# One ordered list of small steps for the prelude and the first 16 units of a fused attention and FFN kernel

## The chip, the cores and the metric

The kernel runs on one core of one Trainium2 chip. The time is device microseconds of one execution. Engines are named as in the profile: PE is TensorE (PEld its weight loads), DVE is VectorE, ACT is ScalarE, POOL is GpSimd, SP is SyncE, which here issues the DMAs.

## What is computed

Batch 8, 8 heads, 512 local and 32 global tokens, head size 64; then an FFN over all 8 x 544 tokens, 512 to 2048 to 512, with a leaky activation that has its own slope for every hidden unit.

```python
k_all = concat([k_g, k_l]); v_all = concat([v_g, v_l])
out_g = softmax(scale * q_g @ k_all.T) @ v_all          # 32 global queries see all keys
s_ll  = where(abs(i - j) <= 32, scale * q_l @ k_l.T, -1e9)
s_l   = concat([scale * q_l @ k_g.T, s_ll])             # local: a window, and the 32 global keys
out_l = softmax(s_l) @ concat([v_g, v_l])
x = concat([out_g, out_l])                              # heads side by side: 512 columns
h = x @ w_in
g = maximum(h, 0) + alpha * minimum(h, 0)
out = g @ w_out
```

## The kernel before

**Units.** The FFN runs in groups of tokens: eight local groups of 512 tokens, one for each batch, and one of the 256 global tokens. A group is worked in 16 units, one for each block f of 128 hidden units. Unit T does `f1(T)`: 12 matmuls of 128x512 that make h for its block, then g (ACT takes the negative part, VectorE combines: "bend"), then a high part gh (ACT, rounded to fp32r) and a low part gl (POOL). `f2(T, 0)` multiplies gh with both parts of the weights (8 matmuls), `f2(T, 1)` multiplies gl with the high part (4 matmuls), both into four banks of PSUM, `LAG` = 2 units later. All operands of the FFN are split like this into a high and a low part.

**Weights.** They come as 64-bit floats, 1 MB for a block f, and are decoded on the chip once, during the first 16 units: `take_high` and `take_low` on ACT, `shift` (two instructions) and `join` (two) on VectorE, then `upper` on ACT (the rounded high part) and `lower` on VectorE (the rest). Unit f of the first group needs `lower(f)`. Three buffers of 128x1024 (`dec`) hold what is being decoded: one from `take_high` to `lower`, one from `take_low` to `join`.

**Attention.** Its local part goes by pairs of heads P, four pairs for each batch: `local_scores` on PE, `local_maxima` on VectorE, `local_exps` on ACT, `local_transposes` on PE with copies of the result, `local_values` on PE, `local_weights` (division by the sum) on VectorE, `local_outputs` (transposes) on PE. Pairs 0 to 3 make x of the first group and stand in a prelude. Pairs 4 to 7 make x of the second group and lie between the first group's units. From pair 8 on (`NRAW`) the transposition goes through a VectorE block transpose and DRAM instead (`local_exchange`). Global attention starts in the second group.

**What orders the work.** A planner orders the instructions by due times from its own timeline. PE's instructions are kept in program order throughout; those of ACT and VectorE are kept in it up to the end of the first group (`act.on`, `vec.on`), the DMAs of the start until `dma.on = False`. So in the prelude and the first group the program text is the order: first the prelude's calls one after the other (lines 542 to 595), then the loop of line 596, where each unit emits f1, g, the f2 of two units before, and the decode steps of later units (lines 612 to 620), and where `attention(t, where)` emits what was planned for that place. `keep_warm(n)` issues n matmuls on zeros into a bank of their own.

**Buffers that matter.** `st`: 21 tiles of 128x512 for x, g, p and so on. PSUM: two banks `h` (f1, values, outputs), two banks `s`, four banks `o0` to `o3` (scores in the prelude, f2 afterwards).

Of the kernel before, what the change touches and what calls it, by code (L numbers as in the profile page):

```python
# [18 lines left out]
NPAIR = 4  # L19
# [14 lines left out]
PAD = (64, 32)  # L34
LAG = 2
NRAW = 2 * NPAIR
NLOAD = 6
# [34 lines left out]
def longformer_ffn(ctx: ExitStack, tc: tile.TileContext, qk, vs, gn, vg, w, alpha, out):  # L72
# [45 lines left out]
    idle = stage("idle", F32R)  # L118
    vec.memset(idle.bitcast(F32), 0.0)
# [20 lines left out]
    def keep_warm(n, tag="s"):  # L140
        for _ in range(n):
            ps = bank(tag, "warm")
            matmul(ps, idle[:, 0:128], idle, start=True, stop=True)

    wslot, wmid, wts = {}, {}, {}
# [12 lines left out]
    def take_high(f):  # L158
        if f < NF:
            wmid[f] = [wide("wt"), None]  # L160
            act.activation(wmid[f][0], words(f)[1].bitcast(F32), AF.Abs)

    def take_low(f):
        if f < NF:
            wmid[f][1] = wide("wr", I32)
            act.activation(wmid[f][1], words(f)[0], AF.Copy, scale=2.0**-29)

    def shift(f):
        if f < NF:
            t = wmid[f][0]  # L170
            vec.tensor_scalar(t, t, CLAMP_LO, CLAMP_HI, op0=ALU.max, op1=ALU.min)
            tu = t.bitcast(U32)
            vec.tensor_scalar(tu, tu, 3, 0x3FFFFFFF, op0=ALU.logical_shift_left, op1=ALU.bitwise_and)

    def join(f):
        if f < NF:
            t, r = wmid[f]
            tu, ti = t.bitcast(U32), t.bitcast(I32)
            vec.scalar_tensor_tensor(tu, words(f)[1], 0xC0000000, tu, op0=ALU.bitwise_and, op1=ALU.bitwise_or)
            vec.tensor_tensor(ti, ti, r, op=ALU.add)  # L180
            del wslot[f]
            wmid[f] = t
# [35 lines left out]
    ps_of, pr_of, z_of, pt_of, xq_of = {}, {}, {}, {}, {}  # L218

    def local_scores(P):  # L220
        t = qks.pop(P)
        tags = ("o0", "o1", "o2", "o3") if P < NPAIR else ("s", "s", "s", "s")
        for h in range(2):
            ps_of[P, h] = bank(tags[2 * (P % 2) + h], "s_ps")
            if P < NRAW:
                matmul(ps_of[P, h], ident_bf, mask_bf, start=True, stop=False)
        for j in range(NWIN):
            c, wd = divmod(j, 4)
            i = place(P, c, wd)
# [21 lines left out]
    def local_exps(P):  # L251
        z_of[P] = small("z", 8)
        for h in range(2):
            src, mn, scale = ps_of.pop((P, h))
            p = pr_of[P, h] = stage("p") if P < NRAW else pr_of[P, h]
            for i in range(4):
                k = 2 * i + h
                act.activation(p[:, 128 * i : 128 * i + 128], src[:, i], AF.Exp, bias=mn[:, i : i + 1], scale=scale, accum_out=z_of[P][:, k : k + 1])

    def local_transposes(P):  # L260
        ps = {}
        for h in range(2):
            p = pr_of.pop((P, h))
            ps[h] = bank("s", "pt")
            for i in range(4):
                transpose(ps[h][:, 128 * i : 128 * i + 128], p[:, 128 * i : 128 * i + 128], ident)

        def put():
            for h in range(2):
                pt_of[P, h] = stage("pt")  # L270
                copy("d" if P < NPAIR else "a", pt_of[P, h], ps[h])

        if P < NPAIR:
            return put
        put()
# [22 lines left out]
    def local_values(P):  # L298
        o = bank("h", "o_ps")
        v = vws.pop(P)  # L300
# [8 lines left out]
    def local_weights(P):  # L309
        o, z, rz = ps_of.pop(P), z_of.pop(P), small("rz", 8)  # L310
        act.activation(rz, z, AF.Copy, bias=1e-9)
# [8 lines left out]
    def local_outputs(P):  # L320
        xq = xq_of.pop(P)
        ps = bank("h", "xt")
        for i in range(4):
            transpose(ps[:, 128 * i : 128 * i + 128], xq[:, 128 * i : 128 * i + 128], ident)
        if P < NPAIR:
            return lambda: xs.update({(0, P): split(ps, SL)})
        act.copy(x_raw[:, P % NPAIR], ps)
# [16 lines left out]
    def global_scores(k):  # L344
# [11 lines left out]
        m, z = small("gm", 4), small("gz", 4)  # L356
# [52 lines left out]
    gs, obs = {}, {}  # L409

    def f1(T, after=None, between=None):
        G, f = divmod(T, NF)
        n = SL if GROUPS[G][0] == "l" else NB * SG
        h = bank("h", "h_ps")
# [9 lines left out]
        g = stage("g")  # L424
        act.activation(g[:, 0:n], h[:, 0:n], AF.Relu, scale=-1.0)
        vec.scalar_tensor_tensor(g[:, 0:n], g[:, 0:n], beta_sb[:, f : f + 1], h[:, 0:n], op0=ALU.mult, op1=ALU.add)
        if between is not None:
            between()
        gh, gl = stage("gh", F32R), stage("gl", F32R)
        act.copy(gh[:, 0:n], g[:, 0:n])  # L430
        nc.gpsimd.tensor_tensor(gl[:, 0:n], g[:, 0:n], gh[:, 0:n].bitcast(F32), op=ALU.subtract)  # L431
        gs[T] = (gh, gl)

    def f2(T, part):
# [6 lines left out]
        gh, gl = gs[T]  # L441
        for m in range(NC):
            ms = slice(128 * m, 128 * m + 128)
            if part == 0:
                matmul(o[m][:, 0:n], wts[f, 1][:, 0, ms], gh[:, 0:n], start=(f == 0), stop=False)
                matmul(o[m][:, 0:n], wts[f, 1][:, 1, ms], gh[:, 0:n], start=False, stop=False)
            else:
                matmul(o[m][:, 0:n], wts[f, 1][:, 0, ms], gl[:, 0:n], start=False, stop=(f == NF - 1))
        if part == 0:
            return  # L450
        del gs[T]
# [24 lines left out]
    turn = {4: 0, 5: 3, 6: 6, 7: 9, 8: 12}  # L476
    for P in range(NPAIR, NPR):
        u = turn.setdefault(P + 1, 4 * (P - NPAIR))
        plan(u, "post", values, P)
        if P == NPAIR:  # L480
            plan(0, "post", scores, P)
            plan(0, "end", local_maxima, P)
            plan(1, "act", local_exps, P)
            plan(2, "pre", local_transposes, P)
        if P < NRAW:
            plan(u, "end", local_weights, P)
            plan(u + 2, "pre", local_outputs, P)
        if P + 1 < NPR:
            plan(u, "post", scores, P + 1)
            if P < NRAW:  # L490
                plan(u, "end", local_maxima, P + 1)
                plan(u + 1, "act", local_exps, P + 1)
                if P + 1 < NRAW:
                    plan(u + 2, "pre", local_transposes, P + 1)
                else:
                    plan(u + 1, "end", local_exchange, P + 1)
            plan(turn[P] + 1, "post", load_qk, P + 1)
            plan(u + 1, "post", load_v, P + 1)
    step = [16 * b + r for b in range(1, 6) for r in (2, 6, 10)] + [98, 106]
# [13 lines left out]
    loaded = [0]  # L513

    def load_next(n):
        while loaded[0] < min(n, NF):
            load_weights(loaded[0])
            loaded[0] += 1

# [5 lines left out]
    load_next(1)  # L525
# [4 lines left out]
    load_next(2)  # L530
    load_v(2)
    load_v(3)
    load_next(3)
    load_qk(NPAIR)
    load_v(NPAIR)
    load_next(4)
    dma.on = False

    def outputs(P):
        local_outputs(P)()  # L540

    keep_warm(8)
    local_scores(0)
    local_scores(1)
    local_maxima(0)
    local_exps(0)
    local_maxima(1)
    take_high(0)
    local_exps(1)
    keep_warm(4)  # L550
    put = local_transposes(0)
    shift(0)
    put()
    take_low(0)
    join(0)
    local_scores(2)
    local_values(0)
    local_maxima(2)
    local_weights(0)
    put = local_transposes(1)  # L560
    put()
    local_exps(2)
    upper(0)
    outputs(0)
    lower(0)
    local_scores(3)
    local_maxima(3)
    local_values(1)
    local_exps(3)
    local_weights(1)  # L570
    put = local_transposes(2)
    put()
    outputs(1)
    take_high(1)
    shift(1)
    take_low(1)
    put = local_transposes(3)
    put()
    join(1)
    keep_warm(2)  # L580
    local_values(2)
    local_weights(2)
    upper(1)
    outputs(2)
    lower(1)
    keep_warm(2)
    local_values(3)
    local_weights(3)
    take_high(2)
    keep_warm(2)  # L590
    outputs(3)
    take_low(2)
    shift(2)
    join(2)
    take_high(3)
    for t in range(NT + LAG):
        u = t + HPU
        with boost(u):
# [11 lines left out]
        if t >= LAG:  # L610
            f2(t - LAG, 1)
        if t < NF:
            load_next(NLOAD + t)
            take_low(t + 3)
            attention(t, "act")
            lower(t + 2)
            take_high(t + 4)
            shift(t + 3)
            join(t + 3)
            attention(t, "end")  # L620
        act.on = vec.on = t + 1 < NF
# [57 lines left out]
```

## Time and profile before

| | |
|---|---|
| runs | 960.09, 952.35 and 950.42 us, median 952.35 |
| profiled execution | 960.0 us, span 958.2 us, granted clock 0.971 |
| busy, share of the span | PE 94%, PEld 76%, DVE 47%, ACT 40%, POOL 20% |
| unit 0's first matmul, unit 15's, unit 16's | 45.91, 183.96, 189.40 us after the span's start |

The span runs from the first to the last instruction. In the views by stage, "x" counts instructions, and the clock column is the TensorE clock that was granted, 1.00 being full speed. In the timeline a row is: start, length, engine, line, operation, output <- inputs, count, and in brackets the idle time before it with what ended it. In the view of waits a row is: who waited for whom, us in total, times, the longest. Line 65 is the helper through which ACT, VectorE and SP instructions are issued, line 96 the one for matmuls, line 99 the one for transposes.

### The profile page before, as it was taken

The numbers are of one execution on the slowest core, as the hardware profiler recorded it, in microseconds if no ns is written. First come the engines' busy times: TensorE is split into PE (matmuls) and PEld (weight loads), VectorE is DVE, ScalarE is ACT, GpSimd is POOL, SyncE is SP. The second block draws the span as 40 slices with busy tenths as digits, with TensorE's granted clock in tenths as the row PEclk, the third lists the DMA queues.
The fourth block names the chain that finished last, engine by engine and source line by source line (L and its number), as shares of the span: only waits on it lengthen the run. The fifth ranks groups of instructions, "written<-read, shape, count | busy, mean of one in ns | idle before, by whom it ended". The sixth has DMA issues, their size and how long they took to land.

```text
span 958.2 us, 21214 instructions
## 1 busy us (share of the span) xinstructions
PE 902.0 (94%) x8672; PEld 728.9 (76%) x8674; DVE 447.5 (47%) x826; ACT 385.8 (40%) x1075; POOL 189.6 (20%) x174
## 2 busy tenths in 40 slices
PE   7657897889999999999999999999999999999998
PEld 4446676667878777877787787877887888888897
DVE  5679777643444444445445454443444333111211
ACT  5456466433334343434334333434343333222222
POOL 3012122111122221212221212222121212222221
PEclk9779988889999999999999999999999999999999
DMA  9845431454554555456554755365545530100010
GB/s 321 308 160 205 150 133 63 160 156 159 173 188 128 180 177 191 140 164 209 183 184 132 229 174 171 116 211 173 192 140 163 174 108 25 44 1 1 1 44 23
DMA packets 139953, 140.33 MB, mean 146 GB/s; under 512 B 9296, under 2 KB 112208, under 8 KB 137808
## 3 DMA queue, kind: packets, MB, share of 16 engines
q1 hardware_dynamic: 139856, 138.98, 43.9%
q8 instruction: 68, 1.11, 0.5%
q14 instruction: 29, 0.24, 0.1%
HBM read 111.16 MB, written 27.79 MB: 145 GB/s over the span
## 4 chain that ended last, share of the span: by engine, by line
PE 77%; DVE 10%; ACT 5%; DMA 4%; issue 1%; SPq 1%; POOL 0%; DVEq 0%; POOLq 0%; ACTq 0%
PE o L96 34%; PE h_ps L96 34%; DVE wt L65 7%; PE o_ps L96 3%; PE s_ps L96 3%; ACT p L65 3%; DMA xb<-xb 2%; DMA pb<-pb 2%; SPq L65 1%; ACT wt L65 1%; DVE mn L65 1%; PE go L96 1%; PE g_ps L96 1%; PE gt L99 1%; ACT wr L65 1%
## 5 line engine op out<-in xcount | busy, mean ns | idle before, releaser
L96 PE MATMUL h_ps<-xh,wt 128*128 128x512 f32 (+1 forms) x1152 | 346.9, 385 | 2.6 <-DVE g L65 2.6
L431 POOL TENSOR_TENSOR gl<-g,gh 128x512 fp32r<-128x512 f32 (+1 forms) x144 | 182.3, 1266 | 760.8 <-ACT gh L65 636.4
L96 PE MATMUL o<-gh,wt 128*128 128x512 f32 (+1 forms) x1152 | 279.7, 385 | 4.3 <-ACT ost L65 4.1
L65 DVE SCALAR_TENSOR_TENSOR g<-g,beta_sb,h_ps 128x512 f32<-128x512 f32 (+1 forms) x144 | 102.3, 711 | 319.6 <-ACT g L65 317.3
L96 PEld LDWEIGHTS h_ps<-xh,wt 128*128 128x128 f32 x1152 | 216.3, 192 | 44.9 <-DVE g L65 2.9
L96 PEld LDWEIGHTS o<-gh,wt 128*128 128x128 f32 x1152 | 206.4, 190 | 50.2 <-issue 6.6
L96 PE MATMUL h_ps<-xl,wt 128*128 128x512 f32 (+1 forms) x576 | 220.6, 383 | 0.0
L65 ACT ACTIVATE g<-h_ps 128x512 f32<-128x512 f32 (+1 forms) x144 | 82.1, 570 | 254.6 <-PE h_ps L96 232.6
L96 PE MATMUL o<-gl,wt 128*128 128x512 f32 (+1 forms) x576 | 152.0, 386 | 0.3 <-issue 0.3
L65 ACT CAST gh<-g 128x512 fp32r<-128x512 f32 (+1 forms) x144 | 85.9, 597 | 132.0 <-DVE g L65 108.2
L96 PEld LDWEIGHTS h_ps<-xl,wt 128*128 128x128 f32 x576 | 110.5, 192 | 21.0
L96 PEld LDWEIGHTS o<-gl,wt 128*128 128x128 f32 x576 | 103.3, 189 | 24.6 <-issue 5.4
L65 ACT ACTIVATE p<-p,mn 128x128 f32<-128x128 f32 x192 | 74.4, 389 | 98.1 <-DVE mn L65 66.8
L65 DVE STREAM_TRANSPOSE pb<-p 128x512 f32<-128x512 f32 x48 | 34.1, 710 | 27.4 <-ACT p L65 27.0
L99 PE MATMUL pt<-ident,p 128*128 128x128 f32 x64 | 15.2, 372 | 26.5 <-ACT p L65 26.4
L96 PEld LDWEIGHTS o_ps<-vw,pt 128*32 128x32 f32 x2048 | 31.3, 113 | 11.3 <-issue 4.7
L96 PE MATMUL s_ps<-qk 64*32 64x128 f32 x2048 | 37.4, 276 | 1.9 <-DMA qk<-in_qk_dram 1.9
L65 DVE TENSOR_TENSOR xq<-o_ps,rz 128x512 f32<-128x512 f32 x32 | 22.1, 692 | 34.7 <-PE o_ps L96 23.8
L65 DVE TENSOR_SCALAR wt<-wt 128x1024 f32<-128x1024 f32 (+1 forms) x32 | 36.2, 1131 | 3.8 <-ACT wt L65 3.3
L96 PE MATMUL o_ps<-vw,pt 128*32 128x64 f32 x2048 | 36.6, 225 | 0.0
L65 ACT ACTIVATION_READ_ACCUMULATOR p<-p,mn 128x1 f32 x192 | 35.9, 187 | 0.0
L96 PEld LDWEIGHTS s_ps<-qk 64*32 64x32 f32 x2048 | 28.8, 106 | 8.0 <-DMA qk<-in_qk_dram 3.3
(79 smaller groups left out, 555.8 us busy)
## 6 DMA issues: line engine op xcount, KB each, us to landing
vw<-in_vs_dram SPq DMA_DIRECT2D x64, 512.0 KB, 5.8
qk<-in_qk_dram SPq DMA_DIRECT2D x32, 672.0 KB, 6.6
ws<-in_w_dram SPq DMA_DIRECT2D x16, 1024.0 KB, 8.9
pb<-pb SPq DMA_DIRECT2D x48, 256.0 KB, 2.1
pt<-pb SPq DMA_DIRECT2D x192, 64.0 KB, 2.0
vg<-in_vg_dram SPq DMA_DIRECT2D x32, 320.0 KB, 3.5
gn<-in_gn_dram SPq DMA_DIRECT2D x32, 288.0 KB, 4.3
out_dram<-ost SPq DMA_DIRECT2D x32, 256.0 KB, 3.9
```

The costliest lines, as they stand in the source:

```text
L65: ins = call(*a, **k)
L96: return tc.keep_in_program_order(nc.tensor.matmul(*a, **k))
L99: return tc.keep_in_program_order(nc.tensor.transpose(*a))
L431: nc.gpsimd.tensor_tensor(gl[:, 0:n], g[:, 0:n], gh[:, 0:n].bitcast(F32), op=ALU.subtract)
```

## The change

The prelude and the loop over the first 16 units become one list of 284 words, `ORDER`. A letter is a small step, the number its pair or unit, and `*n` asks for n matmuls on zeros ahead of it. Since each engine runs its own steps in the list's order, the list orders PE, ACT and VectorE together.

- on PE: S scores, T transposes of p, V values, X transposes of the output, F f1, A and B the two parts of f2
- on VectorE: R maxima, N weights, C copies of pt (pair 3 and pairs from 4 on: ACT), y xl, s shift, j join, l lower, g bend, L rest_g, D the exchange of pair 8
- on ACT: E exps (with the sum's epsilon, which stood in `local_weights`), x rounding of x, h take_high, k take_low, u upper, r the negative part of g, H the rounding of g

Also: in the first 16 units gl is made on VectorE, not on POOL. An exp on one column of `beta_sb` is issued at the start, ahead of everything else on ACT. The matmuls on zeros are bf16 and write into the bank of the step that they stand ahead of. The first copies of pt 3 go from VectorE to ACT. At the start weight blocks 0 to 5 are loaded (0 to 3 before, with two placed differently); block f + 6 follows `join(f)`. Two paddings differ: `alpha_sb` by 32 columns, `gz` 16 columns for 4. From unit 16 on the loop is as before.

```diff
-PAD = (64, 32)
+PAD = (32, 32)
-NLOAD = 6
+ORDER = """
+    S0*8 S1 R0 R1 k0 h0 E0 s0 j0 E1 T0*12 S2 C0 V0 u0 R2 T1 N0 E2 S3 l0 X0 C1 R3 h1 V1*2 x0 T2
+    N1 k1 y0 E3 C2 X1*2 s1 V2*2 x1 j1 T3 C3 N2 u1 y1 h2 l1 V3*8 k2 s2 X2 x2 N3 h3 y2 X3*5 j2 x3
+    S4 R4 u2 k3 y3 F0 E4 s3 F1 l2 j3 h4 T4 r0 r1 s4 u3 k4 g0 g1 F2*9 H0 l3 C4 j4 h5 V4 r2 S5 L0
+    k5 s5 u4 A0 g2 H1 j5 H2 B0 F3 R5 u5 k6 L2 A1 E5 L1 l5 B1 N4 l4 h7 S6 h6 s7 F4 r3 R6 g3 E6 A2
+    s6 j6 B2 r4 F5 H3 g4 u6 L3 H4 l6 A3 k7 L4 h8 j7 B3 r5 F6 s8 u7 k8 g5 A4 l7 r6 H5 j8 h9 B4 F7
+    g6 u8 s9 k9 A5 L5 r7 l8 H6 B5 j9 h10 F8 s10 u9 T5 r8 g7 k10 A6 l9 L6 h11 X4 g8 B6 s11 H8 F9
+    x4 H7 L8 C5 L7 j10 V5 r9 T6 N5 k11 A7 g9 u10 j11 C6 X5 B7 x5 S7 H9 l10 k12 L9 F10 h12 R7 u11
+    s12 V6 r10 l11 E7 A8 N6 g10 B8 j12 H10 S8 h13 F11 L10 k13 R8 u12 X6 r11 A9 x6 l12 E8 g11 T7
+    s13 B9 j13 F12 h14 s14 u13 A10 k14 l13 r12 B10 H11 g12 F13 h15 L11 j14 C7 V7 r13 g13 u14 A11
+    N7 k15 l14 X7 B11 s15 x7 H13 F14 H12 j15 A12 L12 u15 r14 l15 B12 g14 F15 D8 L13 A13 r15 H14
+    g15 H15 B13 L15 L14
+"""
...
-    idle = stage("idle", F32R)
-    vec.memset(idle.bitcast(F32), 0.0)
+    idle = halves[:, 1024:1536]
+    vec.memset(idle, 0.0)
+    act.activation(beta_sb[:, 0:1], idle[:, 0:1], AF.Exp)
...
-    def keep_warm(n, tag="s"):
+    def keep_warm(ps, n, add=False):
         for _ in range(n):
-            ps = bank(tag, "warm")
-            matmul(ps, idle[:, 0:128], idle, start=True, stop=True)
+            matmul(ps, idle[:, 0:128], idle, start=not add, stop=not add)
...
+    def local_copies(P):
+        for h in range(2):
+            pt_of[P, h] = stage("pt")
+            copy("a" if P >= NPAIR or P in (3,) else "d", pt_of[P, h], ps_of.pop((P, h)))
...
+    def rest_g(T):
+        n, gl = width(T), stage("gl", F32R)
+        (vec if T < NF else nc.gpsimd).tensor_tensor(gl[:, 0:n], gs.pop(T)[:, 0:n], gh_of[T][:, 0:n].bitcast(F32), op=ALU.subtract)
+        gl_of[T] = gl
...
     load_qk(0)
     load_qk(1)
-    load_next(1)
+    load_weights(0)
     load_v(0)
     load_qk(2)
     load_qk(3)
     load_v(1)
-    load_next(2)
+    load_weights(1)
     load_v(2)
     load_v(3)
-    load_next(3)
+    load_weights(2)
+    load_weights(3)
     load_qk(NPAIR)
+    load_weights(4)
     load_v(NPAIR)
-    load_next(4)
+    load_weights(5)
     dma.on = False
...
+    def first_f1(T, warm):
+        f1(T, warm, (lambda c: split_x(1, c)) if T == NF - 1 else None)
+
+    def first_join(f):
+        join(f)
+        if f + 6 < NF:
+            load_weights(f + 6)
...
+    for word in ORDER.split():
+        word, _, warm = word.partition("*")
+        if word[0] in on_tensor:
+            on_tensor[word[0]](int(word[1:]), int(warm or 0))
+        else:
+            others[word[0]](int(word[1:]))
+    act.on = vec.on = False
+
+    for t in range(NF, NT + LAG):
```

More of the change, by code (lines that the diff above doesn't have):

```diff
@@ L138, in longformer_ffn @@
     nc.gpsimd.memset(og_sb, 0.0)
-    def keep_warm(n, tag="s"):
+    def keep_warm(ps, n, add=False):
         for _ in range(n):
-            ps = bank(tag, "warm")
-            matmul(ps, idle[:, 0:128], idle, start=True, stop=True)
-    wslot, wmid, wts = {}, {}, {}
+            matmul(ps, idle[:, 0:128], idle, start=not add, stop=not add)
+    wslot, wmid, wlow, wts = {}, {}, {}, {}
     def wide(name, dtype=F32):
@@ L159, in take_high @@
         if f < NF:
-            wmid[f] = [wide("wt"), None]
-            act.activation(wmid[f][0], words(f)[1].bitcast(F32), AF.Abs)
+            wmid[f] = wide("wt")
+            act.activation(wmid[f], words(f)[1].bitcast(F32), AF.Abs)
     def take_low(f):
         if f < NF:
-            wmid[f][1] = wide("wr", I32)
-            act.activation(wmid[f][1], words(f)[0], AF.Copy, scale=2.0**-29)
+            wlow[f] = wide("wr", I32)
+            act.activation(wlow[f], words(f)[0], AF.Copy, scale=2.0**-29)
     def shift(f):
         if f < NF:
-            t = wmid[f][0]
+            t = wmid[f]
             vec.tensor_scalar(t, t, CLAMP_LO, CLAMP_HI, op0=ALU.max, op1=ALU.min)
@@ L176, in join @@
         if f < NF:
-            t, r = wmid[f]
+            t, r = wmid[f], wlow.pop(f)
             tu, ti = t.bitcast(U32), t.bitcast(I32)
@@ L181, in join @@
             del wslot[f]
-            wmid[f] = t
     def upper(f):
@@ L216, in load_v, with local_scores @@
             dma.dma_start(vws[P][:, e], src)
-    ps_of, pr_of, z_of, pt_of, xq_of = {}, {}, {}, {}, {}
-    def local_scores(P):
+    ps_of, pr_of, z_of, rz_of, pt_of, xq_of = {}, {}, {}, {}, {}, {}
+    def local_scores(P, warm=0):
         t = qks.pop(P)
@@ L224, in local_scores @@
             ps_of[P, h] = bank(tags[2 * (P % 2) + h], "s_ps")
+            keep_warm(ps_of[P, h], 0 if h else warm)
             if P < NRAW:
@@ L258, in local_exps, with local_transposes @@
                 act.activation(p[:, 128 * i : 128 * i + 128], src[:, i], AF.Exp, bias=mn[:, i : i + 1], scale=scale, accum_out=z_of[P][:, k : k + 1])
-    def local_transposes(P):
-        ps = {}
+        rz_of[P] = small("rz", 8)
+        act.activation(rz_of[P], z_of.pop(P), AF.Copy, bias=1e-9)
+    def local_transposes(P, warm=0):
         for h in range(2):
             p = pr_of.pop((P, h))
-            ps[h] = bank("s", "pt")
+            ps_of[P, h] = bank("s", "pt")
+            keep_warm(ps_of[P, h], 0 if h else warm)
             for i in range(4):
[L266 to L275, printed above, removed]
+                transpose(ps_of[P, h][:, 128 * i : 128 * i + 128], p[:, 128 * i : 128 * i + 128], ident)
+    def local_copies(P):
+        for h in range(2):
+            pt_of[P, h] = stage("pt")
+            copy("a" if P >= NPAIR or P in (3,) else "d", pt_of[P, h], ps_of.pop((P, h)))
     def exchange(src, put, name):
@@ L296, in split, with local_values @@
         return xh, xl
-    def local_values(P):
+    def local_values(P, warm=0):
         o = bank("h", "o_ps")
+        keep_warm(o, warm)
         v = vws.pop(P)
@@ L309, in local_weights @@
     def local_weights(P):
-        o, z, rz = ps_of.pop(P), z_of.pop(P), small("rz", 8)
-        act.activation(rz, z, AF.Copy, bias=1e-9)
+        o, rz = ps_of.pop(P), rz_of.pop(P)
         vec.reciprocal(rz, rz)
@@ L318, in local_weights, with local_outputs, round_x, rest_x @@
             exchange(xq, x_raw[:, P % NPAIR], "xb")
-    def local_outputs(P):
+    def local_outputs(P, warm=0):
         xq = xq_of.pop(P)
-        ps = bank("h", "xt")
+        ps_of[P] = bank("h", "xt")
+        keep_warm(ps_of[P], warm)
         for i in range(4):
-            transpose(ps[:, 128 * i : 128 * i + 128], xq[:, 128 * i : 128 * i + 128], ident)
+            transpose(ps_of[P][:, 128 * i : 128 * i + 128], xq[:, 128 * i : 128 * i + 128], ident)
+    def round_x(P):
         if P < NPAIR:
-            return lambda: xs.update({(0, P): split(ps, SL)})
-        act.copy(x_raw[:, P % NPAIR], ps)
+            xs[0, P] = stage("xh", F32R), stage("xl", F32R)
+            act.copy(xs[0, P][0], ps_of[P])
+        else:
+            act.copy(x_raw[:, P % NPAIR], ps_of.pop(P))
+    def rest_x(P):
+        xh, xl = xs[0, P]
+        vec.tensor_tensor(xl, ps_of.pop(P), xh.bitcast(F32), op=ALU.subtract)
     gns, vgs, sgs, gz = {}, {}, {}, {}
@@ L355, in global_scores @@
             del gns[2 * k + e]
-        m, z = small("gm", 4), small("gz", 4)
+        m, z = small("gm", 4), small("gz", 16)
         sg_sb = sgs[k] = big[0][:, 1152:1728].rearrange("q (h n) -> q h n", h=2)
@@ L407, in split_x, with width, f1 @@
         xs[G, c] = split((x_raw if kind == "l" else x_glb)[:, c, 0:n], n)
-    gs, obs = {}, {}
-    def f1(T, after=None, between=None):
+    gs, gh_of, gl_of, hs_of, obs = {}, {}, {}, {}, {}
+    def width(T):
+        return SL if GROUPS[T // NF][0] == "l" else NB * SG
+    def f1(T, warm=0, after=None):
         G, f = divmod(T, NF)
-        n = SL if GROUPS[G][0] == "l" else NB * SG
-        h = bank("h", "h_ps")
+        n = width(T)
+        h = hs_of[T] = bank("h", "h_ps")
+        keep_warm(h, warm)
         k = 0
@@ L423, in f1, with leak, bend, round_g @@
                 after(c)
[L424 to L434, printed above, removed]
+    def leak(T):
+        n, g = width(T), stage("g")
+        act.activation(g[:, 0:n], hs_of[T][:, 0:n], AF.Relu, scale=-1.0)
+        gs[T] = g
+    def bend(T):
+        n, g, f = width(T), gs[T], T % NF
+        vec.scalar_tensor_tensor(g[:, 0:n], g[:, 0:n], beta_sb[:, f : f + 1], hs_of.pop(T)[:, 0:n], op0=ALU.mult, op1=ALU.add)
+    def round_g(T):
+        n, gh = width(T), stage("gh", F32R)
+        act.copy(gh[:, 0:n], gs[T][:, 0:n])
+        gh_of[T] = gh
+    def rest_g(T):
+        n, gl = width(T), stage("gl", F32R)
+        (vec if T < NF else nc.gpsimd).tensor_tensor(gl[:, 0:n], gs.pop(T)[:, 0:n], gh_of[T][:, 0:n].bitcast(F32), op=ALU.subtract)
+        gl_of[T] = gl
+    def f2(T, part, warm=0):
         G, f = divmod(T, NF)
@@ L440, in f2 @@
         o = obs[G]
-        gh, gl = gs[T]
+        g2 = (gh_of, gl_of)[part][T]
+        keep_warm(o[0], warm, f > 0 or part > 0)
         for m in range(NC):
@@ L444, in f2 @@
             if part == 0:
-                matmul(o[m][:, 0:n], wts[f, 1][:, 0, ms], gh[:, 0:n], start=(f == 0), stop=False)
-                matmul(o[m][:, 0:n], wts[f, 1][:, 1, ms], gh[:, 0:n], start=False, stop=False)
+                matmul(o[m][:, 0:n], wts[f, 1][:, 0, ms], g2[:, 0:n], start=(f == 0), stop=False)
+                matmul(o[m][:, 0:n], wts[f, 1][:, 1, ms], g2[:, 0:n], start=False, stop=False)
             else:
-                matmul(o[m][:, 0:n], wts[f, 1][:, 0, ms], gl[:, 0:n], start=False, stop=(f == NF - 1))
+                matmul(o[m][:, 0:n], wts[f, 1][:, 0, ms], g2[:, 0:n], start=False, stop=(f == NF - 1))
         if part == 0:
             return
-        del gs[T]
+        del gh_of[T], gl_of[T]
         if f == NF - 1:
@@ L474, in values @@
             local_weights(P)
-    turn = {4: 0, 5: 3, 6: 6, 7: 9, 8: 12}
-    for P in range(NPAIR, NPR):
-        u = turn.setdefault(P + 1, 4 * (P - NPAIR))
+    for P in range(NRAW, NPR):
+        u = 4 * (P - NPAIR)
         plan(u, "post", values, P)
[L480 to L487, printed above, removed]
         if P + 1 < NPR:
             plan(u, "post", scores, P + 1)
[L490 to L497, printed above, removed]
             plan(u + 1, "post", load_v, P + 1)
+        if P + 2 < NPR:
+            plan(u + 1, "post", load_qk, P + 2)
     step = [16 * b + r for b in range(1, 6) for r in (2, 6, 10)] + [98, 106]
@@ L511, in attention @@
             fn(P)
[L513 to L518, printed above, removed]
     def boost(u):
@@ L529, in longformer_ffn @@
     load_v(1)
-    load_next(2)
+    load_weights(1)
     load_v(2)
     load_v(3)
-    load_next(3)
+    load_weights(2)
+    load_weights(3)
     load_qk(NPAIR)
+    load_weights(4)
     load_v(NPAIR)
-    load_next(4)
+    load_weights(5)
     dma.on = False
[L539 to L598, printed above, removed]
+    def first_scores(P, warm):
+        local_scores(P, warm)
+        if P >= NPAIR:
+            load_qk(P + 1)
+    def first_values(P, warm):
+        local_values(P, warm)
+        if P >= NPAIR:
+            load_v(P + 1)
@@ new lines, in first_f1 @@
+    def first_f1(T, warm):
[4 more added lines that the diff above has]
+            load_weights(f + 6)
+    on_tensor = {"S": first_scores, "T": local_transposes, "V": first_values, "X": local_outputs, "F": first_f1, "A": lambda T, n: f2(T, 0, n), "B": lambda T, n: f2(T, 1, n)}
+    others = {"R": local_maxima, "E": local_exps, "C": local_copies, "N": local_weights, "x": round_x, "y": rest_x, "D": local_exchange, "h": take_high, "k": take_low, "s": shift, "j": first_join, "u": upper, "l": lower, "r": leak, "g": bend, "H": round_g, "L": rest_g}
@@ L599, in longformer_ffn @@
+    for word in ORDER.split():
+        word, _, warm = word.partition("*")
+        if word[0] in on_tensor:
+            on_tensor[word[0]](int(word[1:]), int(warm or 0))
+        else:
+            others[word[0]](int(word[1:]))
+    act.on = vec.on = False
+    for t in range(NF, NT + LAG):
+        with boost(t + HPU):
             attention(t, "pre")
         G, f = divmod(t + 1, NF)
-        last = NF <= t + 1 < NT and f == 0
         if t < NT:
-            f1(t, (lambda c: split_x(G, c)) if last else None, lambda: upper(t + 2))
@@ L604, in longformer_ffn @@
-        with boost(u):
+            f1(t, 0, (lambda c: split_x(G, c)) if G < len(GROUPS) and f == 0 else None)
+            leak(t)
+            bend(t)
+            round_g(t)
+            rest_g(t)
+        with boost(t + HPU):
             attention(t, "mid")
-        if t >= LAG:
-            f2(t - LAG, 0)
-        with boost(u):
+        f2(t - LAG, 0)
+        with boost(t + HPU):
             attention(t, "post")
[L610 to L620, printed above, removed]
@@ L621, in longformer_ffn @@
-        act.on = vec.on = t + 1 < NF
+        f2(t - LAG, 1)
     assert not at
```

## The prediction

> **What bounds the kernel now.** I read the page first, then busy time by stage, cut where the PE timeline shows unit 0's first MATMUL (45.91), unit 15's (183.96) and unit 16's (189.40).
>
> ```profile
> 0.00:45.91 45.91, 29.86 (x585) 20.70 (x587) 27.33 (x49) 22.03 (x79) 7.32 (x30) 0.89 0.95 328
> 45.91:183.96 138.05, 108.72 (x972) 85.12 (x970) 107.97 (x118) 81.67 (x171) 24.57 (x15) 0.86 0.42 149
> ...
> 189.40:250.00 60.60, 56.51 (x538) 44.91 (x537) 24.87 (x61) 20.31 (x64) 11.13 (x9) 0.94 0.49 158
> 250.00:958.20 708.20, 701.45 (x6560) 573.64 (x6558) 283.61 (x594) 259.26 (x757) 145.57 (x120) 1.00 0.42 134
> ```
>
> Columns after the length: PE, PEld, DVE, ACT, POOL busy, then granted clock, DMA share, GB/s. From 250 on, PE works 701 of 708 us at clock 1.00: nothing to win there. Units 0 to 14 are different: of 138 us PE is busy 108.7 at clock 0.86 and DVE 108.0; neither is full. The two waits of that stage that tell most:
>
> ```profile
> PE pt L99 <- ACT p L65: 26.4, 8, 10.8
> ...
> DVE g L65 <- ACT g L65: 19.0, 5, 5.3
> ```
>
> And one such gap on PE, with the steps behind it:
>
> ```profile
> 116.17 0.60 PE L99 MATMUL xt<-ident,xq 128*128 128x128 f32 x4
> 121.42 1.12 PE L99 MATMUL pt<-ident,p 128*128 128x128 f32 x4 [4.65 <-ACT p L65]
> ...
> 123.58 1.20 PE L96 MATMUL h_ps<-xh,wt 128*128 128x512 f32 x2
> ...
> 128.00 1.98 PE L96 MATMUL o<-gh,wt 128*128 128x512 f32 x8
> ...
> 130.72 0.62 PE L96 MATMUL h_ps<-xh,wt 128*128 128x512 f32 x2
> ...
> 133.44 1.98 PE L96 MATMUL o<-gh,wt 128*128 128x512 f32 x8
> 135.34 1.10 PE L96 MATMUL o_ps<-vw,pt 128*32 128x64 f32 x64
> ...
> 138.00 1.19 PE L96 MATMUL o<-gl,wt 128*128 128x512 f32 x4
> ```
>
> The engines take turns: PE stands at the transposes of p until ACT has done the exps, which stand behind DVE's maxima, which stand behind the weight decode; then DVE waits for g. That is a matter of order, not of engine time. Each gap is paid twice: two matmuls take 1.20 us behind it and 0.62 at full clock.
>
> **The change, part by part.** The list replaces the turn-taking, so the question is how much work the fullest engine has. Durations are start to start, since an instruction's end overlaps the next.
>
> ```profile
> 14.47 1.42 DVE L65 TENSOR_SCALAR wt<-wt 128x1024 f32<-128x1024 f32 x2 [2.90 <-ACT wt L65]
> 15.81 1.28 DVE L65 COPY pt<-pt 128x512 f32<-128x512 f32 x2
> 17.01 1.22 DVE L65 SCALAR_TENSOR_TENSOR wt<-ws,wt 128x1024 uint32<-128x1024 uint32 x1
> ...
> 19.51 0.68 DVE L65 TENSOR_REDUCE mn<-s_ps 128x4 f32<-128x512 f32 x1
> ...
> 21.11 0.20 DVE L65 RECIPROCAL rz<-rz 128x8 f32<-128x8 f32 x1
> ...
> 22.01 1.28 DVE L65 COPY pt<-pt 128x512 f32<-128x512 f32 x2
> 24.85 0.69 DVE L65 TENSOR_TENSOR xl<-xt,xh 128x512 fp32r<-128x512 f32 x1 [1.55 <-ACT xh L65]
> 25.45 1.22 DVE L65 TENSOR_TENSOR wt<-wt 128x1024 fp32r<-128x1024 f32 x1
> 26.59 0.68 DVE L65 TENSOR_REDUCE mn<-s_ps 128x4 f32<-128x512 f32 x1
> ...
> 117.52 0.75 DVE L65 SCALAR_TENSOR_TENSOR g<-g,beta_sb,h_ps 128x512 f32<-128x512 f32 x1
> 118.19 1.22 DVE L65 TENSOR_TENSOR wt<-wt 128x1024 fp32r<-128x1024 f32 x1
> ...
> 172.11 0.68 DVE L65 SCALAR_TENSOR_TENSOR p<-s_ps,mask 128x512 f32<-128x512 f32 x1
> ...
> 174.75 0.74 DVE L65 SCALAR_TENSOR_TENSOR g<-g,beta_sb,h_ps 128x512 f32<-128x512 f32 x1
> ```
>
> DVE prices: shift 1.34 (14.47 to 15.81), two pt copies 1.20, join 2.50 (17.01 to 19.51), maxima 1.60, reciprocal with xq 0.90, xl 0.60, lower 1.14, g 0.67, pair 8's maxima 2.64 (172.11 to 174.75).
>
> ```profile
> 109.39 1.81 POOL L431 TENSOR_TENSOR gl<-g,gh 128x512 fp32r<-128x512 f32 x1 [5.59 <-ACT gh L65]
> ```
>
> ```profile
> 109.96 2.52 DVE L65 TENSOR_SCALAR wt<-wt 128x1024 f32<-128x1024 f32 x2
> ```
>
> **Lower parts of g.** On POOL each takes 1.81 us and lies across a shift, which then takes 2.52 and not 1.42. On DVE it has the shape of the xl step: I take 0.61 (bounds 0.60, and POOL's 1.81), and the shift gets its 1.1 us back. Net 0.5 us a unit saved on DVE. The new wait: L on DVE waits for ACT's gh, with all of DVE's list behind it; in most units the list sets other work between bend and L.
>
> **When unit 0 starts.** It needs the xl of pair 3 (y3). On DVE y3 now stands behind s2 N3 y2 j2 R4, and s2 waits for the third weight block.
>
> ```profile
> 24.69 1.44 SPq L65 DMA_DIRECT2D ws<-in_w_dram  x1
> ```
>
> ```profile
> ws<-in_w_dram SPq DMA_DIRECT2D x1, 1024.0 KB, 7.8
> ```
>
> The second row is the answer for that issue alone: 24.69 + 7.8 = 32.5, and no load ahead of it on SP's queue changes. Then take_high on ACT, 1.05 (I take DVE's lower of the same size, 1.14, as 1.1), and on DVE 1.34 + 0.90 + 0.60 + 2.50 + 1.60 + 0.60 = 7.5, with 0.3 for hand-overs: F0 at **41.4** (now 45.91), and with three units shifted and joined by then, where now it is two. One more weight block goes ahead of qk 4 and two ahead of vw 4, about 3 us each at the first stage row's 328 GB/s. By hand count S4 is then due at 37 to 38 and V4 not before 52, so both hide: nothing charged; without that cover, 3 us. take_high(1) can hold x0, k1 and E3 behind it on ACT until block 1 lands; that is inside the chain above, which ends later.
>
> PE waits about 2.4 us for y3 right before F0, and no warm matmul stands there. I take F0 at full clock; at half clock, as in the row at 123.58, it takes 2.7 us more, of which the 2 us of warm matmuls before F2 would absorb most. (The Trainium skill, TensorE: Matmul & The Clock Gate, section HAM oscillation, asks for no idle gap over about 3.4 us: the 4.65 us gap above agrees, and by it this gap costs nothing if the work before it was dense, up to the 2.7 us if it counts as idle.)
>
> **From F0 to F15.** DVE after y3 up to l15, which F15 needs: 13 shifts 17.4, 13 joins 32.5, 14 lowers 16.0, 14 g 9.4, 13 L 7.9, R5 to R7 4.8, R8 2.64, N4 to N7 3.6: **94.3 us**. PE: 15 F of 2.72 (130.72 to 133.44) 40.8; 13 A with B of 2.72 (128.00 to 130.72) 35.4; four V with S of 2.66 (135.34 to 138.00) 10.6; four X of 0.60 2.4; four T, taken as two X each, 4.8; nine warm ones 2: **96.0 us**. ACT keeps the 81.7 us of its stage row, 85% of that. PE and DVE are both full, so the ideal is 41.4 + 96.0 = 137.4. I followed the list by hand with these prices: each F finds its lower ready, the two h banks and the three decode buffers come free in time, though some only just; no large wait is built in. Small ones are:
>
> ```profile
> DVE wt L65 <- ACT wt L65: 2.5, 6, 0.5
> ```
>
> Lower now waits up to 0.5 us for ACT; eight of those that the other engine doesn't cover make 4 us (bounds 0, and rival 1). F15 at **141.4** against 183.96: -42.6.
>
> **The boundary.** D8, the exchange of pair 8, moves from unit 13 to behind F15's four splits.
>
> ```profile
> 177.72 0.71 DVE L65 STREAM_TRANSPOSE pb<-p 128x512 f32<-128x512 f32 x1 [1.10 <-ACT p L65]
> ...
> 183.71 3.19 DVE L65 TENSOR_TENSOR xl<-x_raw,xh 128x512 fp32r<-128x512 f32 x4 [1.26 <-ACT xh L65]
> ```
>
> ```profile
> 184.59 1.73 SPq L65 DMA_DIRECT2D pt<-pb  x4
> ```
>
> ```profile
> DMA to landing us min/median/max: 1.8/1.9/2.0
> ```
>
> From its first transposition to the last pt landing: 184.59 + 1.73 + 1.9 - 177.72 = 10.5 us. Behind the splits (3.2 us after F15 starts) it is ready at F15 + 13.7; PE reaches V8 after F15, A13, B13, F16 and A14, at about + 10. PE waits **3.5 us** where it waited for nothing (bounds 0 and 13.7 - 8.2, if A14 is put behind V8).
>
> The rest: the table load goes under the wait for the first loads, but k0 and h0 now stand before E0, so the first exps come no sooner; no gain. Copying pt 3 on ACT takes 1.2 us off DVE before F0, beside the chain. Warm matmuls fill PE gaps ahead of F0. The pads and the wider gz shift addresses; no row shows what that does: I take nothing, and as bounds 1% either way, the spread of the three runs.
>
> **Sum.** 960.0 (profiled execution; 958.2 span and 1.8 around it) - 42.6 + 3.5 = **921**. The profiled execution is 7.65 over the median of 952.35. Since PE is pinned at full clock from 250 on, part of that surplus probably sits in the early stage that is replaced; I carry over half: **917**.
>
> **Rivals.**
> 1. *Hand-overs stay the bound.* F waits for lower, lower for ACT's upper, upper for the join.
>
> ```profile
> 101.42 2.95 DVE wt L65 x2
> ...
> 108.82 2.94 DVE wt L65 x2
> ```
>
> The chain of waits has two lowers 7.4 us apart. If every unit kept that, with the pairs' DVE work beside it (four of 2.5, and 1 more for R8), the stage takes 13 x 7.4 + 11 = 107: F15 at 149, 928 by the profiled sum. For it: PE and DVE have no slack. Against: the list puts s, R and N between j and l. Chance 0.17.
>
> 2. *Slower: the clock.* If PE's gaps recur before the full clock is granted, the 96 us run at half: F15 at 233, so 49 more plus the 3.5: about 1005 by the median. It decides once gaps like that at 121.42 (4.65 us) come more often than the 6.6 us that recovery took (121.42 to 128.00). Against: by hand the list leaves no gap over 2.5 us from F0 on. Chance 0.02.
>
> 3. *What follows is sorted differently* by the planner, or the address shift bites: the 769 us from 189.40 on move by up to 8 us either way. Only the 4 us idle between 189.40 and 250 could be won. Chance 0.08.
>
> 4. *The list does not take hold*: an entry that waits for a buffer holds its whole engine, and the turn-taking comes back: 945 to 955. The early stage is pinned on PE, ACT and DVE, so a wrong due time anywhere in the list is enough. Chance 0.03.
>
> **Numbers.** The forecast, 902 to 924, has 0.70. The low end: no slip and no wait at V8 (137.4 for F15: 913.4), less all of the 7.65, is 906, less a little for rival 3. The high end is rival 1 with part of the address bound: 902 to 934. Within 1% is about what this kernel's runs can tell from no change: faster 0.95, same 0.03, slower 0.02.
>
> **What would show it.** Unit 0 at 41 to 43; F15 at 137 to 145; every shift pair at 1.4; PE and DVE over 90% busy between, at clock 1.00; no wait of PE for p over 2 us; 3 to 4 us before V8. It is wrong if DVE waits over 0.5 us before lower in every unit, if a weight block lands after its take_high is due, or if the stage from 250 on changes.

## The result and the profile after

| | before | after |
|---|---|---|
| median of 4 runs | 956.22 us (950.42 to 961.49) | 919.01 us (916.62 to 923.11) |
| profiled execution, span | 960.0, 958.2 us | 917.19, 915.4 us |
| unit 0, unit 15, unit 17 start on PE | 45.91, 183.96, 197.18 | 41.58, 139.96, 158.05 |

The ratio is 0.9617 (0.9538 to 0.9695). The forecast was 917, its range 902 to 934. The kernel before has a fourth run here, hence the other median. In the sessions of the experiments, where the clock of every run is on record, its runs lie in two clusters, 950 to 955 us at a mean granted clock of 0.976 to 0.980 and 957 to 962 at 0.965 to 0.971, and the profiled one is of the second.

Busy time by stage after, cut at F0, F2 and F15 as the timeline shows them (columns as before; lines 77, 108 and 111, in some runs 76, 107 and 110, are the helpers that were 65, 96 and 99):

```profile
41.58:52.91 11.33, 8.47 (x45) 6.15 (x42) 11.06 (x17) 10.68 (x27) 0.00 (x0) 1.00 1.00 422
52.91:139.96 87.05, 87.05 (x873) 69.88 (x871) 83.13 (x109) 67.91 (x140) 0.00 (x0) 1.00 0.48 169
sum 98.38, PE 95.52 PEld 76.03 DVE 94.19 ACT 78.60 POOL 0.00; mean PE 47.76 PEld 38.01 DVE 47.09 ACT 39.30 POOL 0.00
```

```profile
0.00:41.58 41.58, 33.05 (x667) 19.46 (x674) 29.18 (x51) 26.30 (x85) 7.27 (x30) 0.96 1.00 348
...
250.00:915.40 665.40, 660.41 (x6099) 542.27 (x6098) 264.10 (x553) 243.87 (x703) 138.56 (x115) 1.00 0.40 132
```

The stage that took 138.05 us takes 98.38, with PE 97% and DVE 96% busy at clock 1.00. Of the 39.7 us, 26.5 are idle time of PE (29.3 before, 2.9 after), and 13.2 are its busy time (108.7 and 95.5) for about as much matmul work, at clock 1.00 instead of 0.86: each gap was indeed paid twice. The stage has two parts: up to F2, DVE is full (11.06 of 11.33 us); from F2 on, PE is (87.05 of 87.05). The last stage is as it was, PE-bound. The waits of the whole stage, longest first:

```profile
ACT wt L77 <- DVE wt L77: 11.5, 11, 2.3
ACT g L77 <- PE h_ps L108: 5.3, 5, 2.0
PEld L108 <- issue: 3.5, 3, 3.0
PE h_ps L108 <- DVE g L77: 2.8, 1, 2.8
...
DVE wt L77 <- ACT wt L77: 0.8, 2, 0.5
...
DVE g L77 <- ACT g L77: 0.4, 2, 0.2
```

Of PE's 26.4 us behind p nothing is left, and DVE's 19.0 behind ACT's g are 0.4. Only ACT still waits at length, and ACT is not the bound. The group of DVE's shifts (shortest, median, longest in ns):

```profile
L77 DVE TENSOR_SCALAR wt<-wt x32: 683/694/696, 12.9 to 134.3; 128x1024 f32<-128x1024 f32 x16, 128x1024 uint32<-128x1024 uint32 x16
```

Before, the same row read 683/695/1797. Two places on PE's timeline cost something, F2 and V8:

```profile
47.32 1.03 PE L111 MATMUL pt<-ident,p 128*128 128x128 f32 x8
51.16 2.10 PE L108 MATMUL h_ps<-x_glb 128*128 128x512 bf16 x8 [2.80 <-DVE g L77]
52.91 0.81 PE L108 MATMUL h_ps<-xh,wt 128*128 128x512 f32 x2
...
148.64 1.98 PE L108 MATMUL o<-gh,wt 128*128 128x512 f32 x8
150.54 0.32 PE L108 MATMUL o_ps<-vw,pt 128*32 128x64 f32 x8
153.37 0.99 PE L108 MATMUL o_ps<-vw,pt 128*32 128x64 f32 x56 [2.51 <-DMA pt<-pb]
154.29 1.07 PE L108 MATMUL s_ps<-qk 64*32 64x128 f32 x55
156.66 0.42 PE L108 MATMUL s_ps<-qk 64*32 64x128 f32 x9 [1.30 <-issue]
```

The matmuls on zeros ahead of F2 write into F2's own bank, so they wait for g0 to free it and then stand ahead of F2: they don't fill that gap. The gap is one that the prediction did not have (by hand, none over 2.5 us from F0 on). Ahead of V8, PE waits for the pt of pair 8, as forecast.

Line by line the 42.8 us of span are: F15 44.0 us earlier; from F15 to F17 4.9 us given back (18.09 us where it was 13.22); 3.7 us won after F17, in small steps at the group boundaries. PE's waits after F17 add up to 4.5 us where they were 6.0, which is 1.5 of the 3.7; the cause of the rest stays open.

### The profile page after: what moved, and what is told of

It is laid out like the page before. It is cut to its first block, busy times and chain, and to the rows that moved or that the text cites. A ratio compares the mean times of both kernels' runs of the same rounds, so it can differ in the third digit from the quotient of the medians.

```text
span 915.4 us, 21219 instructions
## 1 busy us (share of the span) xinstructions
PE 890.9 (97%) x8696; PEld 718.8 (79%) x8704; DVE 438.6 (48%) x840; ACT 388.1 (42%) x1078; POOL 163.1 (18%) x158
## 4 chain that ended last, share of the span: by engine, by line
PE 90%; DVE 4%; DMA 2%; issue 1%; ACT 1%; SPq 1%; DVEq 0%; ACTq 0%
PE o L108 40%; PE h_ps L108 39%; PE o_ps L108 4%; PE s_ps L108 4%; DVE wt L77 2%; PE go L108 1%; PE g_ps L108 1%; SPq L77 1%; DMA ws<-in_w_dram 1%; DMA pb<-pb 1%; PE gt L111 1%; DVE xl L77 0%; PE pt L111 0%; PE gx L108 0%; ACT p L77 0%
## 5 line engine op out<-in xcount | busy, mean ns | idle before, releaser
L108 PE MATMUL h_ps<-xh,wt 128*128 128x512 f32 (+1 forms) x1152 | 339.9, 378 | 0.0
L464 POOL TENSOR_TENSOR gl<-g,gh 128x512 fp32r<-128x512 f32 (+1 forms) x128 | 155.8, 1217 | 744.6 <-ACT gh L77 689.2
L108 PEld LDWEIGHTS h_ps<-xh,wt 128*128 128x128 f32 x1152 | 212.2, 188 | 41.8 <-issue 0.6
L108 PE MATMUL h_ps<-xl,wt 128*128 128x512 f32 (+1 forms) x576 | 217.9, 378 | 0.0
L108 PEld LDWEIGHTS h_ps<-xl,wt 128*128 128x128 f32 x576 | 108.4, 188 | 20.3 <-DVE xl L77 0.3
L108 PEld LDWEIGHTS s_ps<-qk 64*32 64x32 f32 x2048 | 29.2, 107 | 10.1 <-issue 7.2
L77 DVE TENSOR_TENSOR xl<-x_raw,xh 128x512 fp32r<-128x512 f32 x28 | 21.5, 814 | 20.5 <-ACT xh L77 17.3
L77 DVE SCALAR_TENSOR_TENSOR p<-s_ps,mask 128x512 f32<-128x512 f32 x48 | 30.1, 665 | 1.3 <-PE s_ps L108 1.3
```

Source lines behind the costliest of these rows:

```text
L77: ins = call(*a, **k)
L108: return tc.keep_in_program_order(nc.tensor.matmul(*a, **k))
L464: (vec if T < NF else nc.gpsimd).tensor_tensor(gl[:, 0:n], gs.pop(T)[:, 0:n], gh_of[T][:, 0:n].bitcast(F32), op=ALU.subtract)
```

## The experiments

Medians are set against the changed kernel's 919.01. The runs come from several sessions; the kernel before was run in each of them and took 950 to 962 us in all. "Stage" is F0 to F15 in the profiled run: 98.4 in the changed kernel, and 100.0 to 101.1 in the three runs below that leave the list from F0 to F14 alone (without the early exp, D8 moved, and D8 with both sent first). So single stages differ by up to 3 us; most of that is the clock at F2 (see "The clock").

**The order alone, and gl alone.** First the same steps in the order of the kernel before:

```diff
-    S0*8 S1 R0 R1 k0 h0 E0 s0 j0 E1 T0*12 S2 C0 V0 u0 R2 T1 N0 E2 S3 ...
+    S0*8 S1 R0 E0 R1 h0 E1 T0*4 s0 C0 k0 j0 S2 V0 R2 N0 T1 C1 E2 u0 ... F0 r0 g0 u2 H0 L0 S4 k3 l2 h4 s3 j3 R4 F1 ...
```

> The changed kernel with the same 284 steps in the order of the kernel before; gl on VectorE, early exp table, early loads and bf16 warm matmuls stay. Theory (the order is what pays): F15 back near 180, PE again waits over 20 us for p, total 945 to 960. Rival (the edits beside the order pay, gl on VectorE above all, since it gives each shift 1.1 us back): under 935.

Measured: 946.91 us (944.17 to 951.49, 10 runs), 0.9917 (0.9884 to 0.9951) of before.

```profile
40.80:172.51 131.71, 102.55 (x971) 80.46 (x970) 102.27 (x131) 81.53 (x168) 0.00 (x0) 0.92 0.44 162
```

```profile
PEld pt L110 <- ACT p L76: 28.9, 8, 11.3
PE pt L110 <- DVE wt L76: 24.9, 4, 10.9
```

The second row's 24.9 us are the same stand at the transposes of p, put down to another releaser. F15 is at 172.5, earlier than the 180 expected: F0 came 5.1 us sooner than in the kernel before, and the stage is 6.3 us shorter, PE's busy time alone by 6.2, at clock 0.92 instead of 0.86. Then with gl on POOL as well:

```diff
-        (vec if T < NF else nc.gpsimd).tensor_tensor(gl[:, 0:n], ...
+        nc.gpsimd.tensor_tensor(gl[:, 0:n], ...
```

> As the one above, and gl on POOL again in the first 16 units. Theory: as the kernel before, 945 to 962, and within 6 us of the one above, because on VectorE L stands between bend and lower and costs there about what the shift gets back. Rival (gl on VectorE pays by itself): 10 us or more slower than the one above.

Measured: 952.68 us (946.25 to 956.45, 10 runs), 0.9967 (0.9933 to 1.0002): the kernel before, rebuilt from the list's steps. The difference of the medians is within the interval, but the two sets of runs hold the two clocks in other proportions. At like clock the kernel before and this one have medians of 951.7 and 948.0 us (0.98), and of 958.2 and 953.5 (0.97), and the runs do not overlap. So all edits but the order and gl (loads, exp table, bf16 zeros, pt 3, pads) are worth about 4 us together; F0 starts at 42.07 where it was 45.91. Its stage has the length of the run above:

```profile
42.07:173.60 131.53, 102.45 (x971) 80.48 (x970) 107.60 (x117) 80.68 (x168) 23.88 (x14) 0.92 0.43 156
```

The medians of the two runs differ by 5.8 us, but at like clock by 1.4 (946.6 and 948.0) and 2.2 (951.3 and 953.5), and the two profiled runs by 0.8. In the old order gl on VectorE is worth 1 to 2 us, hardly more than these runs can tell. In the new order:

> The changed kernel with gl on POOL in the first 16 units, list unchanged but for L. Theory: VectorE loses up to 1.1 us for each shift that a gl crosses and wins 0.61 for each L; since it has 94 us of work in 98, F15 comes 3 to 7 us later, total 921 to 927. Rival (PE alone is the bound): no change, 917 to 920.

Measured: 925.04 us (923.52 to 926.63), 6.0 more, inside what the theory gave.

```profile
40.35:144.58 104.23, 98.21 (x915) 75.98 (x911) 95.74 (x111) 76.93 (x165) 22.01 (x13) 0.98 0.52 191
```

```profile
L77 DVE TENSOR_SCALAR wt<-wt x32: 678/694/1669, 12.2 to 139.0; 128x1024 f32<-128x1024 f32 x16, 128x1024 uint32<-128x1024 uint32 x16
```

Shifts that meet a gl take longer again, now up to 1.67 us. Of the 37 us, then, the order gives about 28 (946.9 to 919.0) and the other edits about 4. The worth of gl depends on the order: 1 to 2 us in the old one, 6 in the new one, where VectorE is full.

**Which half of the order.** Head up to F0 new and the rest old, and the reverse:

```diff
+    (new order up to F0) F0 r0 g0 H0 L0 l2 h4 s3 j3 F1 r1 g1 u3 ... (old order)
+    (old order up to F0) S4 R4 u2 k3 F0 E4 s3 F1 l2 j3 h4 T4 ... (new order)
```

> The changed kernel with the new order up to F0 and the old order of the units from F0 on (the steps that the new order had done already are left out there). Theory (the gain is made between F0 and F15): 940 to 947, that is at most 7 us under the old order's 946.9. Rival (the prelude's order pays, since a third unit is decoded by F0): under 935.

> The other way round: the old order up to F0, then the new order of the rest. Theory: 918 to 926, since F0 comes at about 41 us with either prelude and one unit's decoding, 5 us of VectorE, is still to do. Rival (as above): over 935.

Measured: 941.41 us (939.43 to 944.07) with the new head alone, 924.26 (922.83 to 928.63) with the new rest alone. So the order of the units gives 22.4 to 22.7 of the 28 us, and the prelude's 5.3 to 5.5 on either ground: they add up, and the rival falls.

```profile
40.74:168.60 127.86, 100.64 (x907) 79.38 (x903) 98.84 (x128) 78.97 (x165) 0.00 (x0) 0.92 0.45 165
```

```profile
43.93:147.76 103.83, 98.44 (x917) 77.12 (x912) 96.91 (x127) 79.63 (x169) 0.00 (x0) 0.97 0.50 181
```

An earlier F0 does not show in the new prelude: it starts at 39.2 to 43.1 us in the profiled runs with it, and at 40.8 to 43.9 in the three with the old order and the other edits. What shows is the way from F0 to F2: 15.9 us in the second run here, and 11.3 to 13.0 in those with the whole new list. That fits the unit that is decoded earlier.

**Which engine is full.** Some 9 us of idle work added to one engine at a time, in 13 of the 16 units (`junk` is an unused piece of 128x256):

```diff
+            if f > 2:                                     # in shift, VectorE
+                vec.tensor_tensor(junk, junk, junk, op=ALU.add)   # twice
-  F3 ... F15
+  F3*3 ... F15*3                                          # PE: three matmuls on zeros
+            if f > 2:                                     # in take_high, ACT
+                act.copy(junk, junk)                              # twice
```

> The changed kernel with two idle VectorE additions of 128x256 ahead of each shift from unit 3 on (13 times some 0.75 us, about 9 us of VectorE work in the stage). Theory (PE 95.5 and VectorE 94.2 of 98.4 us: both are the bound): F15 comes 5 to 9 us later, total 924 to 928. Rival (PE alone is the bound): 0 to 3 us later.

> The changed kernel with three matmuls on zeros ahead of each F from unit 3 on (13 times some 0.65 us, about 8.5 us of PE work). Theory (both are the bound): 6 to 9 us later, total 924 to 928. Rival (VectorE alone is the bound): 0 to 3 us later.

> The changed kernel with two idle ACT copies of 128x256 behind each take_high from unit 3 on (13 times some 0.7 us, about 9 us of ACT work). Theory (ACT has 78.6 us of work in 98.4 and is no bound): 0 to 4 us later, through hand-overs alone, total 918 to 922. Rival (the hand-overs through ACT set the pace): 7 us or more.

Measured: 928.59 (927.10 to 930.91), 929.07 (926.96 to 930.24) and 919.33 us (919.21 to 920.64). The stages, in the same order:

```profile
42.97:150.28 107.31, 98.76 (x917) 76.41 (x912) 103.05 (x150) 78.28 (x166) 0.00 (x0) 0.98 0.49 181
```

```profile
43.09:151.52 108.43, 105.60 (x955) 79.31 (x951) 96.10 (x126) 79.15 (x169) 0.00 (x0) 0.98 0.50 181
```

```profile
42.39:142.55 100.16, 97.37 (x917) 76.79 (x912) 94.37 (x125) 86.88 (x191) 0.00 (x0) 0.98 0.54 197
```

DVE's busy time rose by 8.9 us over the changed kernel and the total by 9.6; PE's by 10.1 (1.7 of it the clock at F2, see "The clock") and the total by 10.1; ACT's by 8.3 and the total by 0.3. The first two are slightly above the 928 expected at most. PE and DVE are both the bound, and these 8.3 us on ACT are free: both rivals of the single bound fall, and so does that of the hand-overs through ACT.

**The clock.**

```diff
-    S0*8 ... T0*12 ... V1*2 ... V3*8 ... X3*5 ... F2*9
+    S0 ... T0 ... V1 ... V3 ... X3 ... F2
```

> The changed kernel without any of the matmuls on zeros. Theory (they stand in PE's gaps and the clock at F0 is the most they can give): the prelude's matmuls run at half clock, F0 comes 0 to 3 us later, F0 and F1 perhaps slow, F15 within 4 us of the changed kernel: 918 to 923. Rival (the clock gate decides this stage): 10 us or more slower.

Measured: 920.32 us (918.32 to 923.94), no difference that these runs can tell.

```profile
46.05 1.03 PE L110 MATMUL pt<-ident,p 128*128 128x128 f32 x8
49.82 0.74 PE L107 MATMUL h_ps<-xh,wt 128*128 128x512 f32 x2 [2.74 <-DVE g L76]
...
51.83 1.06 PE L107 MATMUL h_ps<-xh,wt 128*128 128x512 f32 x2
```

The prelude's clock fell to 0.83 (0.88 to 1.00 in the runs with them), but F0 did not come later (40.38). Without the nine ahead of it F2 starts 9.4 us after F0 instead of 11.3 and then runs partly at half clock (two matmuls 1.06 us instead of 0.62): it comes to the same. So the matmuls on zeros decide nothing here.

They take longer in the other runs than in the profiled run of the changed kernel. The stretch of the nine, there and in the run with D8 moved:

```profile
51.16:52.91 1.75, 1.70 (x8) 0.80 (x9) 1.75 (x3) 1.57 (x4) 0.00 (x0) 1.00 0.98 413
```

```profile
52.35:55.79 3.44, 3.22 (x9) 1.21 (x9) 3.30 (x4) 2.72 (x5) 0.00 (x0) 0.50 1.02 426
```

Both follow a gap of 2.8 us. Eight profiled runs have it at 2.73 to 2.83 us, and in seven of them the clock behind it is 0.50 to 0.67; the 1.00 of the changed kernel's profile is the exception. The clock so costs the stage 1 to 2 us in most of these executions, far from the 10 us or more of the rival.

**The exp table.**

```diff
-    act.activation(beta_sb[:, 0:1], idle[:, 0:1], AF.Exp)
```

> The changed kernel without the exp that is issued first. Theory (ACT waits for the first weight block until 10.7 us anyway): one table load of 1.28 us, under that wait if the first copy brings it, ahead of E0 if the exp does; total 918 to 921. Rival: the copy and the exp load a table each, 1.3 us or more on the path, 921 or more.

Measured: 917.07 us (916.86 to 918.42): no loss, and 0.9 us under what the theory gave, so the early exp brings nothing. The table is loaded at the start all the same:

```profile
0.75 1.28 ACT L77 ACT_TABLE_LOAD   x1 [0.75 <-PEq L640]
9.52 1.14 ACT L77 ACTIVATE wr<-ws 128x1024 int32<-128x1024 uint32 x1 [7.49 <-DMA ws<-in_w_dram]
```

With k0 first in the list, the one load runs while k0 waits for the weights. In the kernel before it stood at 9.23, behind DVE's first maximum, because the exps came first.

**The boundary.** First D8 moved by one word, then its two block transposes sent out together ahead of the reads:

```diff
-  g14 F15 D8 L13
+  g14 D8 F15 L13
...
     def local_exchange(P):
+        if P == NRAW:                       # pair 8 alone
+            for h in range(2): ...          # transpose and dma.dma_start(spread, blk), both h
+            for h in range(2): ...          # and only then the four reads of each
+            return
```

> The changed kernel with one word moved: D8 ahead of F15, so ahead of its four splits. Theory: the block transposes start 3.2 us earlier, pt lands 3 us earlier, PE waits under 1 us before and in V8 where it waited 2.5 and 1.3, F17 comes 2.5 to 3.5 us earlier, total 915 to 917 against 919. Rival (the wait is SP's order of its queue, not D8's place): unchanged.

> D8 ahead of F15, and in D8 both block transposes are sent out before either is read back, so that the second does not wait on SP behind the four reads of the first. Theory (PE's wait in V8 is the last pt landing, and SP's order makes that late): no wait over 0.5 us in V8, F15 to F17 14 to 15 us where it is 18.1 in the changed kernel and 16.3 with D8 moved alone; total 914 to 917. Rival (the DMAs themselves are late beside the vw and gn loads): as with D8 moved alone, 918.

Measured: 918.02 us (916.32 to 921.02), 0.9606 (0.9560 to 0.9652) of before, which these runs can't tell from the changed kernel; and 915.57 us (912.99 to 916.98, 6 runs), 0.9577 (0.9544 to 0.9611), five of the six below the fastest run of the changed kernel (916.62). SP's issues with D8 moved, and then with both sent first:

```profile
144.13 0.33 SPq L76 DMA_DIRECT2D pb<-pb  x1
146.71 1.75 SPq L76 DMA_DIRECT2D pt<-pb  x4
148.57 2.03 SPq L76 DMA_DIRECT2D pb<-pb  x1
152.34 2.06 SPq L76 DMA_DIRECT2D pt<-pb  x4
```

```profile
143.00 0.92 SPq L76 DMA_DIRECT2D pb<-pb  x2
145.37 4.14 SPq L76 DMA_DIRECT2D pt<-pb  x8
```

F15 to F17 takes 18.1 us in the changed kernel, 16.3 with the first edit and 13.7 with both: no wait in V8 is left. The first edit missed its expectation (V8 still waited 2.3 us): the second half stood on SP behind the four reads of the first, so it was D8's place and SP's order together. Its issue also took 2.03 us where it took 0.36 in the changed kernel; why stays open. The total gains 3.4 us of the 4.4; in that profiled run DVE's copy of an output waits longer at a late group boundary (PE waits 2.1 us there, 0 in the changed kernel).

## Why the prediction was right

- **The bound.** Right: 94.3 us of DVE work forecast and 94.2 busy, 96.0 of PE work forecast and 95.5 busy, in 98.4 us. The two runs with added work show both as the bound; the run with added ACT work shows that ACT's 80% is not.
- **Small stalls.** 4 us taken, 2.9 found (98.4 less 95.5), but not the ones meant: in place of eight small waits of lower for ACT there are two, 0.8 us, and nearly all of the 2.9 is the one wait at F2, which the list followed by hand did not have. That the sizes are near is luck. F15 came at 139.96, forecast 141.4.
- **When unit 0 starts.** The number was right (41.58 for 41.4) by luck, the reason wrong; in other runs with this prelude F0 starts between 39.2 and 43.1. F0 doesn't wait for y3, which is its last operand: the xl of pair 3 was made at 43.48 (below), 2 us behind F0's start, in time for its last block. F0 stood behind X3 and S4 on PE; N3, ahead of both, had waited 1.35 us on DVE for V3, and V3 stood behind its eight matmuls on zeros (33.23 to 36.54).

```profile
37.71 0.69 DVE L77 TENSOR_TENSOR xq<-o_ps,rz 128x512 f32<-128x512 f32 x1 [1.35 <-PE o_ps L108]
...
43.48 0.68 DVE L77 TENSOR_TENSOR xl<-xt,xh 128x512 fp32r<-128x512 f32 x1
```

- **gl on VectorE.** Sized at 0.5 us a unit for DVE, 8 over 16 units; the run with gl on POOL gives 6.0 in the new order. Shift pairs at 1.4 throughout, as forecast.
- **The boundary.** Right in mechanism, mis-sized by 1.4 us: 3.5 forecast, 4.9 given back. The wait for pt was 2.5 and not 3.5; S9 added 1.3 that the profile puts down to issue, F15 to F16 0.5, and the rest, about 0.6, lies around the two waits.
- **The rest.** The pads, the table, the loads and pt 3 were put at nothing. Together, with the bf16 zeros, they are worth about 4 us at like clock (the old order with gl on POOL against the kernel before). The table and the zeros alone show nothing when taken out of the changed kernel; the others were not tested singly.
- **From the profile to the median.** The sum was 921 for the profiled execution, and 917.2 came, by the 3.7 us won after F17, which no step had. Half of the 7.65 us surplus was taken to sit in the early stage. The rebuilt old order speaks for more: its stage takes 131.5 us at clock 0.92 against 138.05 at 0.86, which is 6.5 us. With only the remaining 1.1 us deducted, the forecast of the median would have been 920 (919.0 came). A sum that was too high and a deduction that was too large partly cancelled, which is luck.
- **Rivals.** The hand-overs (a chance of 0.17) did not happen in the list, but the old order still shows them. The list not taking hold did not happen. The clock did in small: the gap at F2, which was to stay under 2.5 us, is 2.80, and behind it most profiled executions lose 1 to 2 us. The third moved the rest by 3.7 us, within its 8.

## What to carry to other kernels

When two engines are each about 80% busy in a stage and wait for each other in turn, add up each engine's work start to start: the fullest one is what a better order can reach, and here the list came within 3% of it. After that the stage costs one for one on both full engines, so further gains must take work off both, or move it to the one with room (ACT here, at least for the 8.3 us tried). Look at the first consumer behind the reordered stage, too: what was moved to the list's end, an exchange by DMA with its queue's order, returned a tenth of the gain.

## What the runs showed of the hardware that was not expected

- One idle gap of 2.74 us on PE was enough for half clock in F2 (two matmuls 1.06 us) in the run without warm matmuls, and gaps of 2.73 to 2.83 us were followed by a granted clock of 0.50 to 0.67 in six further runs. The Trainium skill, TensorE: Matmul & The Clock Gate, section HAM oscillation, names gaps over about 3.4 us; here shorter ones did it. In the profile of the changed kernel one of 2.80 us did not (clock 1.00).
- Matmuls on zeros can't cover a wait for the bank that they write into: the nine ahead of F2 started after its 2.80 us wait and cost 1.75 us more, and 2.6 to 3.4 us where the clock had fallen.
- The table load on ACT did not wait with the copy behind it (0.75 against 9.52 us), where with an exp first it ran only when the maximum was there (9.23 us).
